# The last 64 keys of probability times v go through 128-row tiles instead of 64-row tiles

## The chip, the core and the metric

The kernel runs on one core of a Trainium2 chip. The metric is the device time of one execution in microseconds (us); the time of a kernel is the median of its runs. A difference of about 0.3%, here some 1.4 us, is what a measurement of this kernel can tell from no change.

## The reference

Sliding-window attention feeds two gated feed-forward blocks. Shapes: batch 4, 8 heads, 576 positions, 64 per head.

```python
scores = q @ k.T / 8 + slope_h * -|i - j|,  kept where 0 <= i - j < 128
attn   = softmax(scores)                      # 576 x 576, a band of 128
x      = attn @ v                             # 576 x 64 for each head
h      = relu(x @ w_in);  g = h * sigmoid(conv3(h));   y = g @ w_out
z      = sigmoid(conv5(y)) * (y @ w_val);     out = z @ w_out2
```

Everything is float32, and the kernel keeps that accuracy by splitting operands into a high and a low half and summing three products (high-high, high-low, low-high).

## The kernel before, in words

The work is cut into eight units: for each batch element `b` one unit `u = 0` (query blocks 0 to 3 of 64 positions) and one unit `u = 1` (blocks 4 to 8). For each unit there is attention for four pairs of heads (`attention`, from L490) and then four chains of matrix products (`hidden`, `mixed`, `valued`, `output`, which all call `dense`, L697, and through it `prod`, L693 to L695). The attention of one unit is interleaved with the matrix products of the unit before it.

Nothing is issued in the order in which it is written. Every operation is handed to `Program.add` with an engine, a duration that the author estimates, a priority and the buffers that it reads and writes. `Program.order` then simulates the engines as a list scheduler does, forward and backward in turns, and keeps the shortest of seven orders; each engine gets its instructions in that order. An engine executes its list strictly in order on the chip. So a changed estimate may change the order of every engine's work, although the operations are the same.

Inside `attention` for one pair of heads: scores (L547, tile `pss`), masking and row minimum (L551), exponential (L559), then the probabilities are scaled and split into two float16 halves `p` (L610 and L612, or L607), and turned so that keys stand on the partitions: for `b = 0` by products with a diagonal matrix (L585, evicted at L591 and L593), for `b` of 1 to 3 by two transposing DMAs of the SP queue (L621, `pt<-p`). There is one buffer `p` and there are two buffers `pt`. The values are scaled and split into float16 halves `v`.

The probability-times-v product is made by `do_pv` (the matmul is L653, tile `psx`, one PSUM bank). It runs over the three half-products `parts` and, within each, over tiles of 128 keys. The two heads `h` of the pair are two matmuls with 64 output columns each, which go to the two column halves of the array. For `u = 0` a third has two key tiles: pairs of matmuls over 256 and 128 moving columns. For `u = 1` the keys are 256 to 575, in four tiles of which the last holds 64 keys only: pairs over 128, 256, 128, 64 and 64 columns, where the last pair takes 64 partitions (`kp = 64`, L637) and the others take 128. The host pads v with 64 zero rows, and `zeros` keeps the columns of `p` beside the last 64 keys at zero, so the upper 64 partitions of the last tile of both `v` and `pt` hold zeros.

For `b` of 1 to 3 all three thirds are one operation of the planner; for `b = 0` the first two are one and the third is another (`gr`, L657). The planner's duration for the operation stands in L660: streamed columns at 2.4 GHz plus a constant for each pair of matmuls plus a constant; the mark `.drain` makes the planner add 85 ns at the next other matmul. The product is then evicted by L674 and L676 (or L669) to `x`, the input of `hidden`.

Of the kernel before, what the change touches and what calls it, by code (L numbers as in the profile page):

```python
# [16 lines left out]
B, H, S, D = 4, 8, 576, 64  # L17
# [227 lines left out]
def attention_moe_moe_kernel(  # L245
# [244 lines left out]
    def attention(b, u, p, prio, step):  # L490
# [4 lines left out]
        t0 = k0 // 2  # L495
        tiles = list(range(t0, (j0 + nb - 1) // 2 + 1))
        qk_t, qk = ring_qk.next()
        vr, vrk = V0[p] if V0 and b == u == 0 else ring_vr.next()
        v, vk = ring_v.next()
# [6 lines left out]
        if not (V0 and b == u == 0):  # L506
            sync(lambda: nc.sync.dma_start(
                out=vr[:, 0:nv], in_=vN[b, :, p, t0:t0 + nv, :]),
                early + 11052.0, (), (vrk,), 182.0 * nv)
        half = 128 * (tiles[-1] + 1) > S  # L510
        vkeys = (vrk,)
        vin, v1, v2 = vr[:, 0:nv], v[:, 0, 0:nv], v[:, 1, 0:nv]
        n = 128 * nv
# [19 lines left out]
        if turn:  # L533
            pt, ptk = ring_pt.next()
        groups = [[0, 1], [2, 3]] if nb == 4 else [[0, 1], [2, 3], [4]]
        for gi, g in enumerate(groups):
            gp, sk = ps_s.next()
            a, e = g[0], g[-1] + 1
# [32 lines left out]
            if turn:  # L571
# [16 lines left out]
                s0, sn, st_ = slots[0], len(slots), (slots[1] - slots[0] if len(slots) > 1 else 1)  # L588
# [7 lines left out]
            for i, s, nkey, _ in blk:  # L596
# [4 lines left out]
                if nth_a in (31,):  # L601
                    t, tk = ring_t.next()
                    t = t[:, 0:nkey]
# [13 lines left out]
        if not turn:  # L617
            pt, ptk = ring_pt.next()
# [14 lines left out]
        mms = []  # L633
        for (pq, pv) in parts:
            for t in tiles:
                for (s0, (so, no), (si, ni), oc, oo, oi) in plan[t]:
                    kp = 64 if (half and t == tiles[-1]) else 128  # L637
                    for h in range(2):
                        mms.append((pq, pv, t - t0, s0, so, no, si, ni, oc, oo, oi, kp, h))
        last = {h: max(i for i, m in enumerate(mms) if m[-1] == h) for h in range(2)}  # L640
        first = {h: min(i for i, m in enumerate(mms) if m[-1] == h) for h in range(2)}

        def do_pv(ms):
            r = []
            for i, (pq, pv, ti, s0, so, no, si, ni, oc, oo, oi, kp, h) in ms:
                base = pt[0:kp, pq].rearrange("p a c -> p (a c)")
                lhs = v[0:kp, pv, ti, 64 * h:64 * h + 64]
                o = xp[64 * h:64 * h + 64, :]
                rhs = bass.AP(base.tensor, base.offset + 128 * s0 + 64 * h,
                              [list(base.ap[0])] + [[128 * st_, n_] for st_, n_ in ((so, no), (si, ni)) if n_ > 1] + [[1, 64]])  # L650
                oap = bass.AP(o.tensor, o.offset + oc,
                              [list(o.ap[0])] + [[st_, n_] for st_, n_ in ((oo, no), (oi, ni)) if n_ > 1] + [[1, 64]])
                r.append(nc.tensor.matmul(out=oap, lhsT=lhs, rhs=rhs, start=(i == first[h]), stop=(i == last[h]),  # L653
                                          skip_group_check=True))
            return r

        for gr in ((((0, 0),), ((0, 1),), ((1, 0),)), (((0, 0), (0, 1)), ((1, 0),)), (((0, 0), (0, 1), (1, 0)),))[  # L657
                1 if b == 0 else 2]:
            ms = [(i, m) for i, m in enumerate(mms) if m[0:2] in gr]
            dur = sum(64 * m[5] * m[7] / 2.4 + 27 for _, m in ms if m[-1] == 0) + 7  # L660
            rd = tuple((ptk, q, gi) for q in sorted({g[0] for g in gr}) for gi in range(len(groups))) + tuple((vk, q + 1) for q in sorted({g[1] for g in gr}))
            pg.add("PE", dur, lambda ms=ms: do_pv(ms), pr, rd, (xpk,)).drain = True
        x, xk = ring_x.next()
# [16 lines left out]
        if u == 1:  # L680
            _, _, pxk, px = X[b, 0, p]
# [132 lines left out]
    for p in range(NP):  # L814
        attention(0, 0, p, p * T0 / NP, T0 / NP / 5)
# [10 lines left out]
    def attentions(b, u, base, T):  # L826
        nb = len(BLK[u])
        for p in range(NP):
            attention(b, u, p, base + T * (p / NP * 0.72 + 0.081), T * 0.72 / NP / (nb + 1))
# [12 lines left out]
    t, todo = T0, UNITS  # L842
    for i, (b, u) in enumerate(todo):
        base = t
        for f in steps:
            t = f(b, u, t, rate)
# [84 lines left out]
```

## Time and profile before

| | |
|---|---|
| median of 3 runs | 459.61 us (458.53 to 460.18) |
| the profiled execution | 460.59 us, of which the span from first to last instruction is 458.8 us |
| busy share of the span | TensorE matmuls 97%, TensorE weight loads 91%, VectorE 77%, ScalarE 71%, GpSimd 54% |
| chain of work that ended last, by engine | PE 43%, DVE 18%, ACT 13%, DMA 9%, POOL 6% |

PE is TensorE's matmul row, PEld its weight loads, DVE is VectorE, ACT ScalarE, POOL GpSimd, SP the queue that issues the DMAs. L653 is line 653 of the kernel. A matmul's form is written rows*columns of the array, then the moving operand: `128*64 128x256 f16` takes 128 partitions, 64 output columns and 256 moving columns. The end of a matmul's record is modelled, so successive records overlap; what a matmul costs is read from start to start.

### The profile page before, as it was taken

Reading aid. Unit: us, or ns where it says so; the run is one execution under the profiler, and the core shown is the slowest. Engines: PE = TensorE matmul, PEld = TensorE weight load, DVE = VectorE, ACT = ScalarE, POOL = GpSimd, SP = SyncE. Lnnn points to the kernel's source line nnn. Section 1 sums busy time; section 2 is a strip of 40 time slices with the busy share of each in tenths; the row PEclk is TensorE's granted clock in tenths of the full one; section 3 lists DMA queues with packets and bytes.
Section 4 is the critical chain, followed back from the end, with each engine's and each line's share of the span. In section 5 each row is a group of like instructions: output and inputs, shape, how many; then the busy total and the mean of one; then the engine's idle time right before and its main releaser. Section 6 shows DMA issues by size and latency. Waiting matters only on the chain.

```text
span 458.8 us, 10275 instructions
## 1 busy us (share of the span) xinstructions
PE 444.5 (97%) x3585; PEld 416.4 (91%) x3585; DVE 351.8 (77%) x1019; ACT 323.9 (71%) x938; POOL 247.8 (54%) x402
## 2 busy tenths in 40 slices
PE   7988999999999999999999999999999999999996
PEld 6767889988999999999999999998999999989996
DVE  5798998897997768885979487956968687936490
ACT  3988999865986568675975587766856687657532
POOL 2787889992567426340665337351753266654532
PEclk9999999999999999999999999999999999999999
DMA  8766666339643436558172427293426547460001
GB/s 271 264 221 217 212 209 214 99 94 317 146 102 60 105 89 150 116 118 182 52 131 72 108 87 164 74 183 98 68 55 136 131 106 145 81 105 1 1 1 58
DMA packets 75236, 57.86 MB, mean 126 GB/s; under 512 B 55984, under 2 KB 65968, under 8 KB 75184
## 3 DMA queue, kind: packets, MB, share of 16 engines
q1 hardware_dynamic: 75184, 57.21, 48.5%
q8 instruction: 28, 0.46, 0.4%
q14 instruction: 24, 0.20, 0.1%
HBM read 39.10 MB, written 4.72 MB: 96 GB/s over the span
## 4 chain that ended last, share of the span: by engine, by line
PE 43%; DVE 18%; ACT 13%; DMA 9%; POOL 6%; issue 3%; SPq 0%; ACTq 0%; POOLq 0%; DVEq 0%
PE pm L693 12%; PE pm L694 12%; PE pm L695 11%; DVE gts L353 7%; PE pss L547 4%; PE psx L653 4%; DMA pt<-p 3%; DMA raw<-in_w_out 3%; DVE t L353 2%; POOL g L368 2%; DMA vr<-in_vN 2%; ACT pss L559 2%; ACT p L610 1%; ACT sg L390 1%; ACT t L346 1%
## 5 line engine op out<-in xcount | busy, mean ns | idle before, releaser
L368 POOL TENSOR_TENSOR g<-t,g 128x254 fp32r<-128x254 f32 (+1 forms) x96 | 80.7, 842 | 25.5 <-ACT g L337 21.1
L353 DVE SCALAR_TENSOR_TENSOR gts<-t,cc,gts 128x322 f32<-128x322 f32 (+4 forms) x120 | 78.4, 682 | 10.4 <-ACT gts L346 8.7
L693 PE MATMUL pm<-x,win 128*128 128x256 f32 (+1 forms) x256 | 80.6, 315 | 1.1 <-DVE t L353 0.6
L693 PE MATMUL pm<-g,wout 128*128 128x254 f32 (+1 forms) x256 | 79.7, 311 | 0.0
L694 PE MATMUL pm<-x,win 128*128 128x256 f32 (+1 forms) x256 | 76.2, 298 | 0.2 <-DVE x L676 0.2
L694 PE MATMUL pm<-g,wout 128*128 128x254 f32 (+1 forms) x256 | 76.2, 298 | 0.0
L695 PE MATMUL pm<-g,wout 128*128 128x254 f32 (+1 forms) x256 | 75.8, 296 | 0.0
L695 PE MATMUL pm<-x,win 128*128 128x256 f32 (+1 forms) x256 | 75.8, 296 | 0.0
L353 DVE SCALAR_TENSOR_TENSOR t<-pm,cc,t 128x325 f32<-128x325 f32 (+3 forms) x112 | 56.0, 513 | 11.6 <-ACT t L346 9.0
L339 POOL TENSOR_SCALAR g<-t 128x254 fp32r<-128x254 f32 (+1 forms) x55 | 26.1, 474 | 69.0 <-DVE t L353 34.1
L551 DVE CUSTOM_DVE_ANT_0 pss<-pss,bm 128x192 f32<-128x192 f32 (+2 forms) x144 | 47.8, 337 | 16.3 <-PE pss L547 14.6
L547 PE MATMUL pss<-qk 128*128 128x192 f32 (+2 forms) x288 | 57.6, 323 | 2.6 <-DVE pt L593 2.6
L693 PEld LDWEIGHTS pm<-x,win 128*128 128x128 f32 x256 | 48.2, 188 | 4.4 <-DVE t L353 2.3
L559 ACT ACTIVATE pss<-pss,st 128x192 f32<-128x192 f32 (+2 forms) x108 | 40.6, 376 | 15.3 <-DVE st L551 14.0
L693 PEld LDWEIGHTS pm<-g,wout 128*128 128x128 f32 x256 | 48.2, 188 | 1.4 <-DVE t L353 0.3
L547 PEld LDWEIGHTS pss<-qk 128*128 128x128 f32 x288 | 44.8, 193 | 5.0 <-DVE pt L593 4.5
L612 DVE SCALAR_TENSOR_TENSOR p<-pss,st,p 128x192 f16<-128x192 f32 (+2 forms) x103 | 36.5, 386 | 16.1 <-DMA pt<-p 10.8
L694 PEld LDWEIGHTS pm<-x,win 128*128 128x128 f32 x256 | 48.3, 189 | 0.4 <-DVE x L676 0.4
L695 PEld LDWEIGHTS pm<-g,wout 128*128 128x128 f32 x256 | 48.6, 190 | 0.0
L694 PEld LDWEIGHTS pm<-g,wout 128*128 128x128 f32 x256 | 48.5, 190 | 0.0
L695 PEld LDWEIGHTS pm<-x,win 128*128 128x128 f32 x256 | 48.2, 188 | 0.0
L346 ACT ACTIVATE t<-pm 128x254 f32<-128x254 f32 (+2 forms) x64 | 25.8, 409 | 26.9 <-PE pm L695 26.9
(109 smaller groups left out, 1184.9 us busy)
## 6 DMA issues: line engine op xcount, KB each, us to landing
qk<-in_qk SPq DMA_DIRECT2D x16, 544.0 KB, 3.8
qk<-in_qk SPq DMA_DIRECT2D x16, 384.0 KB, 3.6
raw<-in_w_out SPq DMA_DIRECT2D x12, 512.0 KB, 4.2
raw<-in_w_in SPq DMA_DIRECT2D x8, 512.0 KB, 4.4
vr<-in_vN SPq DMA_DIRECT2D x16, 256.0 KB, 2.9
raw<-in_vN SPq DMA_DIRECT2D x8, 384.0 KB, 4.5
out<-t SPq DMA_DIRECT2D x16, 161.0 KB, 1.9
raw<-in_w_val SPq DMA_DIRECT2D x4, 512.0 KB, 3.9
```

The costliest lines, as they stand in the source:

```text
L339: "POOL": (pool_t(n), lambda: nc.gpsimd.tensor_scalar(hi, src, 1.0, 0.0, op0=ALU.mult, op1=ALU.add))}
L346: how = {"ACT": (act_t(n, psum, ap), lambda: nc.scalar.activation(out=out, in_=in_, func=AF.Copy, scale=scale)), "DVE": (dve_t(n, ap, fast ...
L353: pg.add("DVE", dve_t(n, 0 if isinstance(scalar, float) else 1), lambda: nc.vector.scalar_tensor_tensor(out=out, in0=in0, scalar=scalar, i ...
L368: "POOL": (pool_t(n, True), lambda: nc.gpsimd.tensor_tensor(out=lo, in0=src, in1=hi.bitcast(F32), op=ALU.subtract))}
L547: return [nc.tensor.matmul(out=o, lhsT=q_t[:, i, :], rhs=k_t[:, kc:kc + nkey], start=True, stop=True, skip_group_check=True) for i, o, nke ...
L551: pg.add("DVE", 128 + 1.05 * nkey, lambda i=i, s=s, nkey=nkey: nc.vector.tensor_tensor_reduce(out=s, in0=s, in1=bm[:, p, 192 - nkey:192], ...
L559: pg.add("ACT", act_t(nkey, True, 2), lambda i=i, s=s, to=to: nc.scalar.activation(out=to, in_=s, func=AF.Exp, scale=-1.0, bias=stt[:, 0, ...
L612: pg.add("DVE", dve_t(nkey, 1), lambda i=i, s=s, hi=hi, lo=lo: nc.vector.scalar_tensor_tensor(out=lo, in0=s, scalar=stt[:, 2, i:i + 1], in ...
L653: r.append(nc.tensor.matmul(out=oap, lhsT=lhs, rhs=rhs, start=(i == first[h]), stop=(i == last[h]), skip_group_check=True))
L693: return [nc.tensor.matmul(out=o, lhsT=wh, rhs=hi, start=first, stop=False), nc.tensor.matmul(out=o, lhsT=wh, rhs=lo, start=False, stop=Fa ...
L694: nc.tensor.matmul(out=o, lhsT=wh, rhs=lo, start=False, stop=False),
L695: nc.tensor.matmul(out=o, lhsT=wl, rhs=hi, start=False, stop=last)]
```

## The change

The last key tile of `u = 1` is multiplied over all 128 partitions, as the other tiles are. The variable `half` and the field `kp` go. The planner's estimate of the operation changes with it.

```diff
@@ -507,7 +507,6 @@
-        half = 128 * (tiles[-1] + 1) > S
         vkeys = (vrk,)
@@ -634,17 +633,16 @@
                 for (s0, (so, no), (si, ni), oc, oo, oi) in plan[t]:
-                    kp = 64 if (half and t == tiles[-1]) else 128
                     for h in range(2):
-                        mms.append((pq, pv, t - t0, s0, so, no, si, ni, oc, oo, oi, kp, h))
+                        mms.append((pq, pv, t - t0, s0, so, no, si, ni, oc, oo, oi, h))
...
-            for i, (pq, pv, ti, s0, so, no, si, ni, oc, oo, oi, kp, h) in ms:
-                base = pt[0:kp, pq].rearrange("p a c -> p (a c)")
-                lhs = v[0:kp, pv, ti, 64 * h:64 * h + 64]
+            for i, (pq, pv, ti, s0, so, no, si, ni, oc, oo, oi, h) in ms:
+                base = pt[:, pq].rearrange("p a c -> p (a c)")
+                lhs = v[:, pv, ti, 64 * h:64 * h + 64]
@@ -657,7 +655,7 @@
-            dur = sum(64 * m[5] * m[7] / 2.4 + 27 for _, m in ms if m[-1] == 0) + 7
+            dur = sum(64 * m[5] * m[7] / 2.4 + 2 for _, m in ms if m[-1] == 0) + (120 if len(gr) > 1 else 60)
```

## Rows read from the trace of the kernel before

**Rows 1.** The page, busy time of TensorE and the granted clock by slices.

```profile
PE 444.5 (97%) x3585; PEld 416.4 (91%) x3585; DVE 351.8 (77%) x1019; ACT 323.9 (71%) x938; POOL 247.8 (54%) x402
...
PEclk9999999999999999999999999999999999999999
```

**Rows 2.** Busy time by stretches: us, PE, PEld, DVE, ACT, POOL, clock, DMA share, GB/s.

```profile
40.00:90.00 50.00, 47.86 (x415) 42.69 (x413) 46.02 (x119) 48.62 (x123) 43.47 (x61) 1.00 0.55 186
...
170.00:220.00 50.00, 50.00 (x452) 47.46 (x451) 40.57 (x137) 36.36 (x118) 19.73 (x41) 1.00 0.59 133
...
270.00:320.00 50.00, 50.00 (x451) 47.05 (x449) 36.98 (x129) 34.70 (x113) 23.11 (x46) 1.00 0.58 128
...
372.00:420.00 48.00, 47.54 (x433) 45.24 (x432) 33.33 (x104) 32.69 (x101) 26.65 (x49) 1.00 0.52 100
```

**Rows 3.** Waits of PE: who for whom, us in total, times, longest.

```profile
PE pss L547 <- DVE pt L593: 2.6, 6, 0.8
...
PE psx L653 <- DMA pt<-p: 0.2, 1, 0.2
```

**Rows 4.** The chain of waits: 0 to 120, then 165 to 340, then pieces after 374.

```profile
by line: DMA raw<-in_w_out 12.0%; ACT sg L390 5.4%; DMA raw<-in_vN 4.8%; POOL g L368 3.9%; DVE vmx L444 3.5%; ACT pm L392 3.2%; DVE gts L353 2.9%; DVE t L353 2.5%; issue 2.5%; ACT p L559 2.1%; POOL gts L364 2.1%; POOL wval L368 2.1%; DVE pm
...
by line: PE pm L693 25.3%; PE pm L694 23.4%; PE pm L695 23.2%; PE pss L547 11.1%; PE psx L653 8.5%; DMA vr<-in_vN 3.2%; DVE gts L353 1.7%; ACT vr L518 0.8%; POOL v L521 0.7%; ACT t L346 0.4%; POOL v L339 0.4%; PE psx L478 0.4%; PE psx L464 
...
381.31 4.75 DMA pt<-p
...
406.43 0.39 PE pm L694
```

**Rows 5.** Tile psx, 170 to 220: duration ns min/median/max, first and last start, forms.

```profile
L653 PE MATMUL psx<-pt,v x120: 192/219/273, 181.5 to 212.2; 128*64 128x128 f16 x48, 128*64 128x256 f16 x24, 128*64 128x64 f16 x24, 64*64 64x64 f16 x24
```

**Rows 6.** Timeline of PE, one product of unit 1: start and length in us, first form.

```profile
181.24 0.28 PE L695 MATMUL pm<-g,wout 128*128 128x254 f32 x1
181.45 0.24 PE L653 MATMUL psx<-pt,v 128*64 128x128 f16 x1
...
181.54 0.36 PE L653 MATMUL psx<-pt,v 128*64 128x256 f16 x5
...
181.65 0.39 PE L653 MATMUL psx<-pt,v 128*64 128x128 f16 x5
...
181.70 0.34 PE L653 MATMUL psx<-pt,v 128*64 128x64 f16 x4
...
181.82 0.22 PE L653 MATMUL psx<-pt,v 64*64 64x64 f16 x2
...
181.97 0.25 PE L653 MATMUL psx<-pt,v 128*64 128x128 f16 x2
...
182.49 0.25 PE L653 MATMUL psx<-pt,v 128*64 128x128 f16 x2
...
182.86 0.22 PE L653 MATMUL psx<-pt,v 64*64 64x64 f16 x2
...
183.01 0.39 PE L693 MATMUL pm<-g,wout 128*128 128x254 f32 x1
```

**Rows 7.** Timeline of PE, one product of unit 0, which has no 64-row tile.

```profile
239.15 0.39 PE L653 MATMUL psx<-pt,v 128*64 128x128 f16 x6
...
239.21 0.44 PE L653 MATMUL psx<-pt,v 128*64 128x256 f16 x6
...
239.48 0.22 PE L653 MATMUL psx<-pt,v 128*64 128x128 f16 x2
239.64 0.42 PE L693 MATMUL pm<-g,wout 128*128 128x326 f32 x1
```

**Rows 8.** Timeline of PE, a product of b = 0, unit 1, in two operations.

```profile
57.91 1.11 PE L653 MATMUL psx<-pt,v 128*64 128x128 f16 x20
58.94 0.39 PE L693 MATMUL pm<-x,win 128*128 128x256 f32 x1
...
60.60 0.59 PE L653 MATMUL psx<-pt,v 128*64 128x128 f16 x10
61.12 0.71 PE L585 MATMUL pss<-dg,p 128*128 128x128 f32 x4
```

**Rows 9.** Tile pt: landing times of the transposing DMAs, from issue.

```profile
DMA to landing us min/median/max: 2.9/3.5/5.3
```

## The prediction

> **What bounds the kernel.** I read the page's busy times first, then the busy times by stretches, then who waits for whom, then the chain of waits, and last the timeline of single products. TensorE is busy 97% of the span, and its granted clock never falls below full [rows 1], so the chip's clock plays no part here. The stretches show where that share is a limit. In the two stretches from 170 to 220 and from 270 to 320 us PE is busy for all 50.00 us, while DVE, the next engine, is busy for 40.6 and 37.0 [rows 2]. Over the whole run PE waits for little: its longest sum is 2.6 us, in six waits of the transposes of b = 0 [rows 3]. From 165 to 340 us the chain of work that ended last is almost all PE, and the probability-times-v products alone (psx, L653) are 8.5% of it [rows 4]. Two places differ. Before 120 us the chain runs through weight DMAs, ACT, POOL and DVE [rows 4], and ACT is busy 48.6 of 50 us from 40 to 90 [rows 2]. From 374 us on it runs through DVE, ACT, POOL and a transposing DMA until PE takes over at 406.43 [rows 4]. What PE saves counts fully in the middle, hardly at the start, and partly in the last batch element.
>
> **What the change removes.** In unit 1 each third of a product is five pairs of matmuls, over 128, 256, 128, 64 and 64 moving columns, and the last pair is the only one of form 64*64: 24 of 120 matmuls in the 170 to 220 stretch, which holds four products [rows 5]. In the timeline of one product the pairs of one third start at 181.45, 181.54, 181.65, 181.70, 181.82, and the next third at 181.97 [rows 6]. The steps are 0.09, 0.11, 0.05, 0.12 and 0.15 us. A pair over 128 columns holds the array 0.05 (181.65 to 181.70), so the pair over 64 columns before the 64*64 pair, with a step of 0.12, and the 64*64 pair itself, with 0.15, each hold it far longer than half of that. Each is where the row tiling changes. The three thirds start at 181.45, 181.97 and 182.49, and the next dense matmul at 183.01: 0.52 us each, 1.56 in all [rows 6].
>
> Unit 0 has no 64*64 pair, and its thirds follow without a pause. From 239.15 to 239.48 two thirds of 128 + 256 columns, 768 in all, take 0.33 us, or 0.027 for 64 columns; the step from a 128 to a 256 pair is 0.06 (239.15 to 239.21), where unit 1 pays 0.09; and from the last 128 pair to the first dense matmul are 0.16 us (239.48 to 239.64), of which 0.05 is its own stream, so leaving the product costs about 0.10 [rows 7].
>
> **What a third costs afterwards.** The one price that no row shows is a 64-column pair followed by another pair of the same tiling. Below it cannot be less than the stream, 0.027; above, the nearest row is a 128-column pair, 0.05 to 0.06. I take 0.03, since the 128 and 256 pairs both hold the array for little more than their stream, and keep 0.055 for the range. First third: 0.09 + 0.11 + 0.05 + 0.03 + 0.03 = 0.31. Second: 0.06 + 0.11 + 0.05 + 0.03 + 0.03 = 0.28. Last: 0.06 + 0.11 + 0.05 + 0.03, then 0.03 of stream and 0.10 to leave, 0.38. The sum is 0.97 instead of 1.56: 0.59 us less for each product of three thirds. With 0.055 for the six 64-column pairs it is 0.59 - 0.15 = 0.44.
>
> The Trainium skill has a rule against so small a price: TensorEngine Tiling (Array Packing), section "Instruction Overhead", says that each matmul carries about 60 cycles, so that one column lasts as long as 60. By it, an estimate, the two matmuls of a pair are 120 cycles or 0.05 us, and the gain per product is 0.47 instead of 0.59; the two matmuls of a pair start within 0.01 us of each other in this trace, which speaks against adding them up.
>
> For b = 0 the product is two operations. The one with two thirds takes 57.91 to 58.94, 1.03 us, and would take 0.31 + 0.38 = 0.69; the one with one third takes 60.60 to 61.12, 0.52, and would take 0.09 + 0.11 + 0.05 + 0.03 + 0.13 = 0.41 [rows 8]. That is 0.45 less for each of four products.
>
> **What it adds.** No instruction and no DMA: the number of matmuls is the same, v and p already hold the zeros, and v's last tile is loaded whole before. A pair over 64 columns of 128 partitions exists already beside the new one [rows 5], so 64 more rows cost no columns. No wait is added: the product reads the same buffers as before.
>
> **What it moves.** The planner's estimate for the operation, with L660's formula: three thirds of unit 1 go from 800 + 15 x 27 + 7 = 1212 ns to 800 + 15 x 2 + 120 = 950, and of unit 0 from 480 + 6 x 27 + 7 = 649 to 612. Since every engine's order comes out of that plan, all orders may shift, the SP queue's included. What this is worth I cannot read from a row in either direction: PE's gaps in the stretches of rows 2 bound a gain, 0.46 us from 372 to 420 and 2.1 from 40 to 90; a loss has no such bound. I take nothing for it and put 2 us on the range.
>
> **The sum.** There are 16 products of unit 1, four for each b. Those of b = 1 and b = 2 lie in the two stretches where PE is full and is the chain: 8 x 0.59 = 4.7 us, all of it kept. Of b = 3, one lies behind 406.43, where PE is the chain again: 0.6 kept. The other three lie between 380 and 406 us beside the chain through DVE and POOL, but PE is busy 47.54 of 48 there [rows 2], so both are nearly in step, and what PE saves becomes a wait unless the new order moves the other engines' work forward. Of their 1.8 us I take half, 0.9, and keep nothing and all as ends. Those of b = 0, 4 x 0.45 = 1.8 us, I cost at nothing, covered by the weight loading on ACT and DMA; without that cover they are a further gain of 1.8. Total: 4.7 + 0.6 + 0.9 = 6.2 us. The profiled execution took 460.59 us (span 458.8 and 1.8 around it) and would come to 454.4; it lies 0.98 above the median of 459.61, which would become 453.4.
>
> **Rivals.**
> - Short pairs cost as much as the 128-column ones, 0.055. For: nothing in the trace shows two short pairs of one tiling in a row. Then the gain is 6.2 x 0.44 / 0.59 = 4.6 us: 455.0. By the rule named above it would be 4.9, or 454.7.
> - PE is not the only bound once it is quicker: DVE at 40.6 of 50 us has bursts, and the last batch element hangs on the DVE chain altogether. If b = 3 keeps nothing and b = 1 and 2 keep three quarters, 3.5 us are gained: 456.1. Against it stands the chain from 165 to 340.
> - The pauses belong to short matmuls rather than to the change of tiling. Then a 64-column pair of 128 rows pauses as well, and the time stays at 459.6. Against it: leaving a product of unit 0 also costs 0.10 behind a 128-column pair [rows 7], so pauses of that size come with another tiling, not with short streams.
> - Slower: PE reaches the products earlier than the turned p. For b = 1 to 3 it comes by two transposing DMAs, each 3.5 us from issue to landing in the median [rows 9], and today PE waits for one only once, 0.2 us [rows 3]. If the new order issues them later or the products sooner, PE, which works strictly in order, stands still with all dense matmuls behind it. The 24 products of b = 1 to 3 hang on such DMAs; the point of no gain is 6.2 / 24 = 0.26 us for each, slower by more than 0.3% is 0.32. With a third of the 3.5 us exposed at ten of them it is 11.7 us: 459.6 - 6.2 + 11.7 = 465.1. Against it: the orders keep the DMAs' distance in the plan, and PE stays nearly in step with it.
>
> **Chances.** The forecast has 0.58, the price of short pairs 0.12, the second bound 0.15, no change 0.07, slower 0.08. Faster by over 0.3%, about 1.4 us and what a measurement can tell, is the sum of the first three, 0.85; within it 0.07; slower 0.08. The range reaches down to 450.5, where b = 0 and all of b = 3 count (8.9 us gained, or 7.1 and 2 from a better order), and up to 456.8, past the second and third case, or the forecast with some 3 us lost to a worse order.
>
> **What would show it.** In the profile after, no 64*64 form is left; a product of unit 1 in one operation takes about 0.97 us from its first start to the next dense matmul; PE's busy time falls by 6 to 9 us. In the stretches of b = 1 and 2 PE is still full, which shows that the time went with it; new waits of PE in the last batch element would show the half that I gave up. I am wrong if the product is short and the time is not (a wait on pt or g in PE's list names the cause), or if the steps around the last pair stay at 0.12 and 0.15.

## The result, and the profile after

The changed kernel takes 462.44 us (median of 8 runs) against 459.6 for the kernel before beside it: a ratio of 1.0057, with an interval of 1.0038 to 1.0076. It is slower by about 2.6 us, where 453.4 us was forecast and 450.5 to 456.8 given as the range. The profiled execution took 460.98 us, with a span of 458.9. Below, times are compared by such ratios to runs of the kernel before on the same chip; 0.1% is 0.46 us.

The products themselves became as short as forecast. The timeline of PE in the changed kernel, one product of unit 1 in one operation (start and length in us, the first form of the group, how many):

```profile
191.99 0.24 PE L651 MATMUL psx<-pt,v 128*64 128x128 f16 x1
...
192.24 0.39 PE L651 MATMUL psx<-pt,v 128*64 128x64 f16 x7
...
192.26 0.37 PE L651 MATMUL psx<-pt,v 128*64 128x64 f16 x6
192.29 0.39 PE L651 MATMUL psx<-pt,v 128*64 128x128 f16 x6
...
192.96 0.38 PE L691 MATMUL pm<-g,wout 128*128 128x254 f32 x1
```

From its first start to the next dense matmul are 0.97 us (191.99 to 192.96), where [rows 6] have 1.56. Ten of the twelve products of unit 1 that are one operation take 0.97 us; behind the other two (1.85 and 1.27) PE waits before its next matmul. The two pairs over 64 columns start at 192.23 (the row at 192.24 is the second matmul of that pair) and 192.26, and the next third at 192.29: 0.03 us each, where the steps were 0.12 and 0.15. The forms of tile psx from 170 to 220 us, for [rows 5]:

```profile
L651 PE MATMUL psx<-pt,v x120: 192/219/273, 183.3 to 212.6; 128*64 128x128 f16 x48, 128*64 128x64 f16 x48, 128*64 128x256 f16 x24
```

The 24 matmuls of form 64*64 are now of form 128*64 128x64. PE's busy time over the span fell by 7.7 us from that of [rows 1], in a span that stayed the same:

```profile
PE 436.8 (95%) x3586; PEld 411.1 (90%) x3586; DVE 358.7 (78%) x1031; ACT 323.3 (70%) x934; POOL 247.6 (54%) x394
```

So the time saved on PE came back as idle time of PE. The stretches of [rows 2], with the same columns (us, then busy time of PE, PEld, DVE, ACT, POOL, then clock, DMA share, GB/s):

```profile
40.00:90.00 50.00, 45.62 (x398) 41.34 (x399) 47.65 (x122) 48.24 (x120) 41.31 (x56) 1.00 0.54 182
170.00:220.00 50.00, 49.34 (x466) 47.70 (x464) 41.27 (x145) 38.06 (x127) 20.23 (x41) 1.00 0.65 140
270.00:320.00 50.00, 49.96 (x470) 48.13 (x470) 40.52 (x148) 36.98 (x125) 24.69 (x47) 1.00 0.67 141
372.00:420.00 48.00, 46.03 (x434) 44.23 (x433) 34.53 (x104) 34.97 (x108) 27.90 (x51) 1.00 0.43 100
```

From 40 to 90 us PE is busy for 2.2 us less than before, from 372 to 420 for 1.5 less. And PE's waits (who for whom, us in total, times, longest), for [rows 3]:

```profile
PE pss L584 <- DVE dg L576: 4.2, 4, 1.7
PE pm L691 <- DVE t L353: 2.3, 3, 1.6
...
PE pm L692 <- POOL g L368: 1.7, 3, 1.0
PE pm L691 <- ACT t L346: 1.4, 1, 1.4
PE pss L584 <- ACT sg L390: 1.0, 1, 1.0
```

None of these five is a wait of the product or of anything that the diff's matmuls touch, and none is for a transposing DMA. The whole list has one wait of the product, 0.3 us for ACT, and no wait for a transposing DMA. They are waits for DVE, POOL and ACT, at products that the change doesn't mention. DVE is busy for 6.9 us more than in [rows 1], over 1031 instructions instead of 1019: the planner, which got other estimates, gave some operations to other engines and another order to all of them.

### The profile page after: what moved, and what is told of

It reads as the page before. It is cut to its first block, busy times and chain, and to the rows that moved or that the text cites. A ratio compares the mean times of both kernels' runs of the same rounds, so it can differ in the third digit from the quotient of the medians.

```text
span 458.9 us, 10268 instructions
## 1 busy us (share of the span) xinstructions
PE 436.8 (95%) x3586; PEld 411.1 (90%) x3586; DVE 358.7 (78%) x1031; ACT 323.3 (70%) x934; POOL 247.6 (54%) x394
## 5 line engine op out<-in xcount | busy, mean ns | idle before, releaser
L339 POOL TENSOR_SCALAR g<-t 128x254 fp32r<-128x254 f32 (+1 forms) x61 | 30.3, 497 | 62.1 <-DVE t L353 35.0
L558 ACT ACTIVATE pss<-pss,st 128x192 f32<-128x192 f32 (+1 forms) x108 | 40.5, 376 | 18.6 <-DVE st L550 15.4
L609 ACT ACTIVATE p<-pss,st 128x192 f16<-128x192 f32 (+1 forms) x103 | 37.0, 400 | 10.1 <-DMA pt<-p 6.0
```

The lines of the kernel that those rows point to most:

```text
L339: "POOL": (pool_t(n), lambda: nc.gpsimd.tensor_scalar(hi, src, 1.0, 0.0, op0=ALU.mult, op1=ALU.add))}
L558: pg.add("ACT", act_t(nkey, True, 2), lambda i=i, s=s, to=to: nc.scalar.activation(out=to, in_=s, func=AF.Exp, scale=-1.0, bias=stt[:, 0, ...
L609: pg.add("ACT", act_t(nkey, True, 1), lambda i=i, s=s, hi=hi: nc.scalar.activation(out=hi, in_=s, func=AF.Copy, scale=stt[:, 2, i:i + 1]), ...
```

## The experiments

The change has two parts, another form of 96 matmuls and another estimate. The theory was that the first is worth what was forecast and that the order that comes out of the second takes it back; the first rival was that PE is no longer the bound, whatever the order.

**The two parts, each alone.** The first kernel is the kernel before with one line edited; each engine's list of instructions is the old one, and only the rows of the last tile differ. The second is the kernel before with only the estimate of the change; in the traces its VectorE, ScalarE and GpSimd execute the same operations in the same order as those of the changed kernel.

```diff
-                    kp = 64 if (half and t == tiles[-1]) else 128
+                    kp = 128
```

> The 128-row matmuls alone, with the planner's old estimate, so that every engine has the list of instructions of the kernel before. Theory A (the shorter products are worth what was forecast, and the new order takes it back): 451.5 to 454.5 us, some 6 us below before, each product of three thirds 0.97 us. Rival B (PE is not the bound once its products are shorter, whatever the order): 458 to 460 us, with new waits of PE that sum to about the 8.6 us saved.

```diff
-            dur = sum(64 * m[5] * m[7] / 2.4 + 27 for _, m in ms if m[-1] == 0) + 7
+            dur = sum(64 * m[5] * m[7] / 2.4 + 2 for _, m in ms if m[-1] == 0) + (120 if len(gr) > 1 else 60)
```

> The old 64-row matmuls with the planner's new estimate, so that the order is that of the changed kernel. Theory A: the new order alone costs about 8 us, and the long products come back on top of it: 466 to 470 us. Rival B: the order costs nothing, 460 to 463 us.

Measured: 454.14 us, a ratio of 0.9904 (0.9875 to 0.9932), for the matmuls alone, and 466.95, 1.0183 (1.015 to 1.0216), for the estimate alone. Both lie where the theory put them, and the rival is out. With the four corners (the two kernels of the change and these two), the new matmuls are worth 0.96% in the old order and 1.26% in the new one (1.0183 - 1.0057); the new order costs 1.53% with the new matmuls (1.0057 - 0.9904) and 1.83% with the old ones. In us of 459.6 that is a gain of 4.4 to 5.8 and a loss of 7.0 to 8.4.

The busy times of the 128-row matmuls in the old order show what the new order costs PE:

```profile
PE 437.4 (97%) x3585; PEld 412.4 (91%) x3585; DVE 352.0 (78%) x1019; ACT 323.5 (72%) x938; POOL 248.0 (55%) x402
```

PE is as busy as in the changed kernel, 437.4 against 436.8 us, but the span is 451.9 instead of 458.9: in the old order PE is idle for 14.5 us, in the changed kernel for 22.1.

How the gain builds up in the old order can be read from the ends of units. The rows are the last `pm<-g,wo` matmul of the first, third, fifth and last unit in the timeline, first of the kernel before, then of the 128-row matmuls in the old order, then of the changed kernel:

```profile
108.07 0.28 PE L695 MATMUL pm<-g,wo 128*128 128x254 f32 x1
...
208.55 0.28 PE L695 MATMUL pm<-g,wo 128*128 128x254 f32 x1
...
307.63 0.28 PE L695 MATMUL pm<-g,wo 128*128 128x254 f32 x1
...
455.07 0.30 PE L695 MATMUL pm<-g,wo 128*128 128x322 f32 x1
```

```profile
106.67 0.28 PE L695 MATMUL pm<-g,wo 128*128 128x254 f32 x1
...
205.62 0.28 PE L695 MATMUL pm<-g,wo 128*128 128x254 f32 x1
...
302.38 0.28 PE L695 MATMUL pm<-g,wo 128*128 128x254 f32 x1
...
448.18 0.30 PE L695 MATMUL pm<-g,wo 128*128 128x322 f32 x1
```

```profile
110.96 0.28 PE L693 MATMUL pm<-g,wo 128*128 128x254 f32 x1
...
207.79 0.28 PE L693 MATMUL pm<-g,wo 128*128 128x254 f32 x1
...
309.51 0.28 PE L693 MATMUL pm<-g,wo 128*128 128x254 f32 x1
...
455.18 0.30 PE L693 MATMUL pm<-g,wo 128*128 128x322 f32 x1
```

In the old order the lead over the kernel before is 1.4, 2.9, 5.3 and 6.9 us: it grows in every batch element, as the products come. (The two profiled executions are 6.9 us apart, the medians 4.5, so these leads are too large as a whole.) The changed kernel is behind that by 4.3 us at the end of the first unit, 2.2 at the end of the third, 7.1 at the end of the fifth and 7.0 at the end.

**Is it the estimate, or this order?** Four more kernels have the changed matmuls and estimates a few ns away from the change's: only the two constants, 120 for an operation of several thirds and 60 for one, are other numbers.

```diff
-            ... + (120 if len(gr) > 1 else 60)
+            ... + (100 if len(gr) > 1 else 50)
```

> The changed kernel with an estimate 20 ns shorter for each operation of two or three thirds and 10 ns shorter for one of one third (constants 100 and 50 instead of 120 and 60). If the loss is the luck of one order, any small shift gives another one: anywhere from 453 to 465 us. If a shorter estimate as such packs PE's list too tight, this is slower than the changed kernel: 462.5 to 464 us.

> The changed kernel with an estimate 20 and 10 ns longer (constants 140 and 70). Luck of the order: anywhere from 453 to 465 us, with no relation to the shorter one. Too tight a plan: faster than the changed kernel, 459 to 461.5 us.

> The changed kernel with the estimate 10 and 5 ns shorter (constants 110 and 55). Luck: anywhere from 452 to 464 us. A rule: between the neighbours 100 (455.5 us) and 120 (462 us).

> The changed kernel with the estimate 10 and 5 ns longer (constants 130 and 65). Luck of the order: anywhere from 452 to 464 us, with no relation to its neighbours 120 (462 us) and 140 (454.9 us). A rule: between these two, 455 to 462 us, and above the median of both.

| constants | median, us | ratio to before | interval |
|---|---|---|---|
| 100 and 50 | 455.53 | 0.9937 | 0.9920 to 0.9955 |
| 110 and 55 | 454.75 | 0.9909 | 0.9880 to 0.9939 |
| 120 and 60 (the change) | 462.44 | 1.0057 | 1.0038 to 1.0076 |
| 130 and 65 | 454.28 | 0.9894 | 0.9870 to 0.9918 |
| 140 and 70 | 454.87 | 0.9925 | 0.9906 to 0.9943 |
| 27 per pair and 7 (the old order) | 454.14 | 0.9904 | 0.9875 to 0.9932 |

Five of six orders bring the 128-row matmuls 0.6 to 1.1% below the kernel before, and one, that of the change, 0.6% above it. Both neighbours, 10 ns away on either side, are at 0.99. The six are different orders: VectorE alone executes from 1019 to 1034 operations in them, and no two have the same number. There is no trend with the constant, so a plan that is too tight is not the cause: the order that came out at 120 is an outlier. For 110 and 130 a rule had been expected as well, a time between the neighbours; both medians lie below both of theirs, so that falls.

The granted clock of TensorE is a further rival, and it has a small part. Over a run it is 0.996 on average in four of the eight runs of the changed kernel and 0.999 to 1.000 in the others, with medians of 462.8 and 462.0 us; the kernel before has 0.998 or more in all 83 runs beside the experiments. But the profiled execution of the changed kernel had the full clock throughout, and its span is still 7.0 us longer than that of the old order. A profile that shows the loss of clock is that of the kernel with the new order up to 98 us and the old one behind it (below):

```profile
PEclk9999899999899999999999999999999999999999
```

There PE stands idle from 48.3 to 50.0 us, works again, and from 51.1 to 54.6 us is granted half the clock (1.2 GHz); the same happens from 122.8 us on, behind a pause from 119.9 to 121.5. The changed kernel's own profile has two pauses of that length, 1.62 us up to 49.29 and 1.72 up to 106.83, and the old order with the same matmuls has none above 1.1 us but the one before PE's first matmul. So a part of what the new order costs, by these runs some 0.4 us of its median, may come by the clock, in some executions and not in others.

**The two largest new waits.** If single waits make that order slow, taking them away within it should show. Two stood out. PE waits 4.2 us for the diagonal matrices from DVE and 1.0 for those from GpSimd, where the rows of the old order with the new matmuls read 0.3 and 1.5:

```profile
PE pss L585 <- POOL dg L578: 1.5, 4, 0.5
...
PE pss L585 <- DVE dg L577: 0.3, 1, 0.3
```

And ACT waits for the loads of v, these rows being from the waits of ACT in the changed kernel:

```profile
ACT vr L517 <- DMA vr<-in_vN: 9.5, 4, 3.1
...
ACT v L523 <- DMA vr<-in_vN: 2.3, 3, 1.5
```

and this one from the old order with the new matmuls:

```profile
ACT vr L518 <- DMA vr<-in_vN: 4.8, 5, 2.2
```

Two kernels change one thing each and keep the order of the plan; the third has both edits, and the fourth has the first in the old order.

```diff
-        vr, vrk = V0[p] if V0 and b == u == 0 else ring_vr.next()
+        vr, vrk = V0[p] if V0 and b == u == 0 else ring_vr.next() if (2 * b + u) * NP + p < 12 or p % 2 == 0 else (ring_sg.t[0].bitcast(F32).rearrange("r (t c) -> r t c", c=128), "vr0")
```

> The changed kernel with every list of instructions as it is, but from the fourth unit on every second load of v goes to another buffer (one of the two of sg, idle by then), so that its DMA no longer waits for the readers of the load before. Theory C (in the new order ScalarE stands before v's scaling until the DMA lands, 11.8 us in seven waits against 4.8 in five in the old order, and tanh and the rest queue behind it until PE waits too): 457.5 to 460.5 us, the waits on in_vN at least halved. Rival D (these waits are covered, the loss is elsewhere): within 1 us of the changed kernel, 461.5 to 463 us.

```diff
+                    dgs.append(pg.add(("DVE", "POOL"), ...))
...
-            o.fn()
+            (o.alts[1][2] if o in dgs else o.fn)()
```

> The changed kernel in its order, but the 17 diagonal matrices (dg) that the plan gives to VectorE are made on GpSimd, at the same place of the order. Theory E (VectorE makes them in 0.27 us alone but in up to 1.6 beside GpSimd, and PE waits 4.2 us for them in four waits, against 0.3 in the old order): 459.5 to 461 us, gained before 112 us. Rival D: within 1 us of the changed kernel, or slower, since GpSimd takes 0.37 for each.

> Both edits in the changed kernel's order. If C and E are separate causes their gains add up: 455.5 to 458.5 us, near the other three orders (454.1 to 455.5). If the start's loss is given back by the middle anyway: no better than the first of the two alone.

> The 128-row matmuls in the old order, which has 4.8 us of waits for v's DMA, with the second buffer. If what those waits cost goes by their sum, 0.5 to 1.5 us less than without it: 452.6 to 453.6 us. If they are covered there: 453.6 to 454.6 us.

The second buffer gave 1.0045 (1.0029 to 1.006) instead of 1.0057, the diagonals on GpSimd 1.0051 (1.0029 to 1.0073), both edits 1.0031 (1.0004 to 1.0058): by these ratios 1.2 us of the 7 at most, and all three intervals overlap with that of the changed kernel. Both expectations of a cause fell. But neither edit took its wait away, so what the two waits cost is not shown. The waits of ACT with two buffers show why the first is small:

```profile
ACT sg L517 <- DMA sg<-in_vN: 3.1, 1, 3.1
ACT vr L517 <- DMA vr<-in_vN: 2.3, 2, 1.9
ACT v L523 <- DMA sg<-in_vN: 1.2, 1, 1.2
```

With half a us on `vr` that isn't shown, 7.1 are left of 11.8 us, where the expectation was half or less, and the 4.7 that went brought 0.6 us by the ratios, which is within their noise. And the first row of PE's waits with the diagonals on GpSimd:

```profile
PE pss L584 <- POOL dg L577: 8.4, 9, 1.5
```

The wait did not go, it moved and grew, from 4.2 us for DVE and 1.0 for GpSimd to 8.4 for GpSimd. In the old order the second buffer made 453.61 us, 0.9866 (0.9846 to 0.9885), the lowest ratio of this study and faster than both the kernel before and the changed one; its interval overlaps with that of the old order without it, and the median lies on the border of the two expectations, so whether those waits cost anything there stays open.

**Where the order loses.** Here the kernel takes the operations in the order of one plan until a time of that plan and what is left in the order of the other, with the 128-row matmuls throughout.

```diff
+    plans = [plan(True), plan(False)]
+    head, tail = plans if OLD_FIRST else plans[::-1]
+    n = next((i for i, h in enumerate(head) if h[3] >= CUT), len(head))
+    done = {h[0] for h in head[:n]}
+    order = head[:n] + [h for h in tail if h[0] not in done]
```

> 128-row matmuls; the order of the old plan until its time 98 us (the end of the first unit's last product), then what is left in the order of the new plan. In the profiles the new order is 4.3 us behind the old one at the end of the first unit, 2.2 at the end of the third and 7.0 at the end of the last. Theory F (the loss at the start is real and stays): without it 462 - 4.3, some 457.5 to 459 us. Theory G (what is lost at the start is made good by the third unit, the loss that counts comes later): 460 to 462 us.

> The reverse: the new plan's order until 98 us, then the old one's. F: 454.1 + 4.3, some 457.5 to 459 us. G: 454.5 to 456 us.

> The old plan's order until 191.5 us of the plan (the end of the third unit), then the new one's. By the profiles 4.8 of the 7.0 us are lost behind that point: 458 to 460 us. If the order's loss were at the start alone: 453.5 to 455.5 us.

> The reverse: the new plan's order until 191.5 us, then the old one's. By the profiles 2.2 us are lost up to that point: 455.5 to 457 us. If all were lost at the start and stayed: 458 us and more.

> 128-row matmuls; the old plan's order until its time 14 us, then what is left in the new plan's order. If the loss of the first unit comes from the order of the first loads (eye and the second load of v's maxima change places, and the second weight load leaves at 12.4 instead of 9.0 us): the first unit's last product ends near 107 us in the profile as in the old order. If it comes later in the unit: near 111 us as in the new one. The total moves by less than in the splice at 98 us: 459.5 to 462 us.

> The same with the splice at 40 us of the plan. If the loss of the first unit lies before 40 us, the first unit's last product ends at 107 to 108 us; if it lies behind (PE waits of 1.2, 0.9 and 2.0 us at 62, 71 and 107 us in the new order), at 109 to 111 us. Total 459 to 462 us.

| splice | old order first | new order first |
|---|---|---|
| at 14 us of the plan | 1.0041 (1.0017 to 1.0065) | |
| at 40 us | 0.9983 (0.9963 to 1.0003) | |
| at 98 us, end of the first unit | 1.0013 (0.9987 to 1.0040) | 1.0009 (0.9986 to 1.0031) |
| at 191.5 us, end of the third | 0.9948 (0.9925 to 0.9971) | 0.9998 (0.9981 to 1.0015) |

The new order's first unit alone, ahead of the old order, costs 1.05% (1.0009 - 0.9904), 4.8 us; all that follows the third unit costs 0.44 to 0.59% (0.9948 - 0.9904, 1.0057 - 0.9998), 2.0 to 2.7 us. By the intervals, such a difference of two ratios is good to some 0.3%, or 1.5 us. The medians are 459.91 for the old order up to 98 us, near theory G, and 459.18 for the reverse, just above F; 457.32 for the old order up to 191.5, between its two expectations, and 458.84 for the reverse, which says that what the new order loses at the start stays lost when the old order follows. So neither theory holds alone. The first unit alone costs 1.05%, everything but the first unit 1.09% (1.0013 - 0.9904), and the sum of the two is more than the 1.53% of the whole: the parts cover each other, or the seam, where one plan's list goes over into the other's, costs something itself. No run here tells the two apart. With the old first unit the first unit ends as early as in the old order, but the third ends where it does in the changed kernel (207.79):

```profile
107.07 0.28 PE L696 MATMUL pm<-g,wo 128*128 128x254 f32 x1
...
207.78 0.28 PE L696 MATMUL pm<-g,wo 128*128 128x254 f32 x1
```

The splices at 14 and 40 us took 461.23 and 458.33 us. Within the first unit, its last product ends at 110.78 us with the splice at 14 us and at 109.31 at 40 us (timeline of these two):

```profile
110.78 0.28 PE L696 MATMUL pm<-g,wo 128*128 128x254 f32 x1
```

```profile
109.31 0.28 PE L696 MATMUL pm<-g,wo 128*128 128x254 f32 x1
```

Against 110.96 with no splice and 107.07 at 98 us, the order of the first loads is worth 0.2 us, that from 14 to 40 us 1.5, and that from 40 to 98 us 2.2. Each of these ends is read from one execution, and four profiles of the old order up to there have it from 106.41 to 107.30, so the 0.2 is nothing and the others are good to about 1 us. The loss is spread over the order, in several pieces of one to three us; no single place was found. Which operations would have to change places is left open.

## Why the prediction was wrong

- **The product: right.** 0.97 us instead of 1.56 was forecast for three thirds and 0.97 was measured. The 64-column pair after a pair of its own tiling, the one price without a row, was taken at 0.03 and is 0.03. The Trainium skill (TensorEngine Tiling (Array Packing), "Instruction Overhead") gives some 60 cycles for each matmul. Added up over the two matmuls of a pair that is, as an estimate from this page, 0.05 us, and the trace of the changed kernel does not agree: two matmuls that go to two halves of the array together held it 0.03 us. One price of 60 cycles for the whole pair, 0.025 us as an estimate from the same page, would fit. The rival that short matmuls pause by themselves is out too.
- **What passes through: a little too much.** In the old order 4.4 us (0.68 to 1.25% of 459.6: 3.1 to 5.7) were gained, against 6.2. By the ends of units in the profiles, good to about 1 us each, the split may also have been another: b = 0, costed at nothing because ACT and the weight loads cover it, gave 1.4 us by the end of the first unit, where three of its four products lie, forecast as 0.45 shorter each. The gains up to the third and fifth unit, 1.5 and 2.3, stand beside three and four products of 0.59, or 1.8 and 2.4, and the last 1.6 beside 2.1.
- **The order: the step that failed.** The text said of the planner's estimate that all orders may shift, that no row tells what this is worth, that a loss has no bound, "I take nothing for it and put 2 us on the range". It was worth 7.0 to 8.4 us, more than the whole forecast gain. The six orders of the same matmuls lie between 0.9894 and 1.0057 of the kernel before, 1.6% or some 7 us; the 2 us put on the range held less than a third of that, and the chances had no case for it. Nothing was a fair middle to take, but its width was guessed and not measured: a few neighbouring estimates would have shown it. That the estimate of the change came out as the one slow order of six is bad luck.
- **The rival of the other sign: right sign, wrong place.** It had PE waiting for the transposing DMAs of p. The changed kernel's list of PE's waits has no such row; the new waits are for DVE, POOL and ACT. The case came with 0.08 on a sign that was right for another reason.
- **What would show it wrong** was named: a short product and no shorter time. PE's busy time fell by 7.7 us, within the 6 to 9 that were named, and that did not make the kernel faster. The wait "on pt or g in PE's list" was there with g at 1.7 us (0.9 in the old order), one of five and not shown to be a cause.

## What to carry to other kernels

Where a planner orders the work, an edit to an estimate is a second change, and the two have to be run apart: here the matmuls alone were 1.0% faster and the estimate alone 1.8% slower. Before a change to such a kernel is judged by one order, try a few estimates a little to either side; a scatter of 1.6% between orders hides any local gain of 1%. And where the other rows can be zeros, try a matmul in the row tiling of its neighbours: here, at 0.1 us for each change of tiling, the two changes in a third cost 0.2 us, beside some 0.27 that its 640 columns take (0.027 for 64).

## What was not expected of the hardware

A small operation of VectorE can last until what GpSimd does beside it ends. In the changed kernel the reciprocal's preparation `st`, of one or two elements for each partition, has a minimum, median and maximum of 140, 297 and 1226 ns on VectorE, and 191, 191 and 513 on GpSimd:

```profile
L561 DVE TENSOR_SCALAR st<-st x26: 140/297/1226, 16.6 to 382.7; 128x2 f32<-128x2 f32 x22, 128x1 f32<-128x1 f32 x4
```

```profile
L563 POOL TENSOR_SCALAR st<-st x54: 191/191/513, 7.1 to 403.3; 128x2 f32<-128x2 f32 x42, 128x1 f32<-128x1 f32 x12
```

A wait of PE of 1.72 us hangs on such a case (timeline of the changed kernel, releasers in brackets):

```profile
104.99 1.26 POOL L368 TENSOR_TENSOR wo<-gts,wo 128x512 fp32r<-128x512 f32 x1
105.05 1.64 DVE L576 TENSOR_SCALAR dg<-eye,st 128x128 f32<-128x128 f32 x1
...
106.19 0.42 POOL L801 MEMSET p<- 128x384 f16 x1
...
106.83 0.35 PE L584 MATMUL pss<-dg,p 128*128 128x128 f32 x1 [1.72 <-DVE dg L576]
```

The diagonal matrix, 0.27 us at its shortest, starts 0.06 us behind a GpSimd operation of 1.26 us and ends 0.44 behind it, which is 0.08 behind the end of the memset that GpSimd does next. That distance comes back: of the 17 diagonals that VectorE makes in this trace, 12 last 0.42 to 1.64 us, and each of them ends 0.08 us (78 to 85 ns) behind the end of a GpSimd operation. The other five last 0.27 to 0.29 us, and one of them, at 52.60 us, lies within a GpSimd operation of 1.3 us; so not every such operation is held up. The Trainium skill says in SBUF — State Buffer, "SBUF: two separate sides", that the two engines share a pair of ports as an exclusive lock for a whole instruction, against VectorE operations in a two-port mode or with two inputs in SBUF, and that the loser blocks. The twelve agree and the one at 52.60 does not; whether these operations meet the page's condition is not shown, and no run here took the GpSimd operation away.
